# Writing out the order of stages 2 and 3 of a two-layer network in single engine steps

## The chip, the cores and the metric

The kernel runs on one core of one Trainium2 chip. The metric is the device time of one execution in microseconds (us). The core has five engines with instruction queues of their own: TensorE (PE: matmuls; PEld: its weight loads), VectorE (DVE), ScalarE (ACT), GpSimd (POOL) and SyncE (SP), which issues every DMA of this kernel. Each engine takes its instructions in the order in which they were put into its program, and an instruction whose input isn't there holds back all that stand behind it.

## What is computed

```python
def _A_ref(x, wqkv, wo):                      # linear attention, 32 heads of 18
    q, k, v = ...(x @ wqkv)
    phi = lambda t: jnp.where(t > 0, t + 1, jnp.exp(t)) + 1e-6
    pq, pk = phi(q), phi(k)
    kv = jnp.einsum("bhsd,bhse->bhde", pk, v)
    z = jnp.einsum("bhsd->bhd", pk)
    num = jnp.einsum("bhqd,bhde->bhqe", pq, kv)
    den = jnp.einsum("bhqd,bhd->bhq", pq, z)[..., None] + 1e-6
    return (num / den) @ wo
def _B_ref(x, w_q, k1, k2, u, v):             # 64 experts, one for each of 32 heads
    s1, s2 = (scores of x against the folded keys of both halves)
    i1, i2 = (the best of 8 in each)
    act = _gelu(x . u[i1 * 8 + i2])
    return sum over the heads of act * v[i1 * 8 + i2]
x = x + _A_ref(_layernorm(x)); x = x + _B_ref(_layernorm(x))
x = x + _A_ref(_layernorm(x)); x = x + _B_ref(_layernorm(x))
```

There are 2,048 tokens of 576 features, in float32. The same weights serve both layers.

## The kernel before

The tokens lie in 16 tiles of 128. All products are made in float32r, with each operand split into a high and a low part: ScalarE copies the high part, VectorE subtracts it (`split`, lines 117 to 120), and three products (high by high, high by low, low by high) are summed in PSUM, so that one product of a tile is 28 matmuls on TensorE. PSUM holds four buffers of two banks (line 70).

The work of a tile is cut into *pieces*, written as Python generators, and each piece into steps by `yield`. A piece has a short name (lines 756 to 775):

- `fT` (lines 300, 210 to 251): transposes the normalized tile for the front. Some tiles are transposed on TensorE (five transposes, then the split). The tiles in `SQUARES` (lines 57 to 61) go another way: VectorE transposes squares of 32, SyncE writes them to DRAM (line 233) and reads them back in four parts (line 239), then comes the split. `oT` (line 468) does the same for the attention's output, with one small GpSimd copy more (line 470), and `bT` (line 508) for the experts' input.
- `k`, `v`, `q` (lines 303 to 330): the front's three products with their evaluation. `keep` stores the transposed tile in DRAM, `rl` loads it back and `lq` makes the q product late (lines 332 to 349). `st` adds a tile's key-value state on TensorE (line 351).
- `mk`, `zs`, `M` (lines 379 to 433): after all 16 tiles, the state is masked and multiplied with the output weights (`wl` loads them).
- `ld` (`ldx`, `ldq`), `num`, `oT`, `O` (lines 436 to 492): load of x and q, division by the denominator, transposition, and the output product of 28 matmuls (line 485) with residual sum (line 475), and layernorm over GpSimd and ScalarE (lines 186 to 208).
- `bT`, `S` (lines 508, 520): transposition, and the experts' scores (14 matmuls of 512 columns, line 527). Its first matmuls need the high part of the transposed tile, its last five the low part. `sel` (line 550) picks the experts on VectorE, `gel` (line 535) makes the gelu on ScalarE and GpSimd.
- `cT`, `po` (lines 511, 600): transposition of the gates, and the experts' output product (four matmuls, line 609). In layer 1 `bc` (line 495) does a `bT` and the `cT` of another tile in one: up to six transposes, then one split for all. `base` (line 593) puts a residual into PSUM on TensorE.

Stage 1 (lines 778 to 858, about the first 148 us) is the front of layer 0 and the folding of the expert weights; its order is given by a loop. Stages 2 and 3 (lines 859 to 923) are written out as a text: `O1.2` means "the next step of piece `O` for layer 1, tile 2", `x3` means three steps, and `bc1.7,6` is the transposition of tile 7's input and tile 6's gates. `play` (line 767) runs such a text, and `in_order` (line 159) then ties each instruction of TensorE, ScalarE, VectorE and GpSimd to the one before it on its engine in the order of the text. The tie holds the order and is no semaphore. SyncE isn't among these: its transfers are put in order by the scheduler of the framework, by its own reckoning.

Of the kernel before, what the change touches and what calls it, by code (L numbers as in the profile page):

```python
# [22 lines left out]
P = 128  # L23
# [13 lines left out]
NB = 5  # L37
# [27 lines left out]
def network(ctx, tc, x_in, wqkv, wo, wq_t, k_t, u_t, v2, c_mask, c_mask4, c_ident, c_code, c_code1, c_scale, c_shift, out):  # L65
# [120 lines left out]
    def spread(xt, total, n):  # L186

        m = wk.tile([P, 2], F32, tag="mv", name=f"m{n}")
        nc.gpsimd.tensor_scalar(m[:, 0:1], total, -1.0 / D, 1.0, op0=ALU.mult, op1=ALU.mult)  # L189
        nc.scalar.activation(junk, xt, AF.Square, bias=m[:, 0:1], accum_out=m[:, 1:2])  # L190
        return m

    def layernorm_sum(xt, m, n):
# [3 lines left out]
        nc.gpsimd.tensor_tensor(rs[:, 1:2], m[:, 0:1], rs[:, 0:1], op=ALU.mult)  # L197
        return normalized(xt, rs, n)
# [11 lines left out]
    def transposed(y, n, more=None, tag="t", step=P):  # L210
# [16 lines left out]
    def moved(y, n, step=P):  # L227
# [3 lines left out]
        nc.vector.transpose(r.rearrange("p (j b c) -> p b j c", j=4, b=NB), at)  # L231
        d = dr.tile([P, NB * P], F32, name=f"y_d{n}")
# [9 lines left out]
    def squares(y, n, step=P):  # L242
        g = yield from moved(y, n, step)
        hi, lo = (wk.tile([P, NB, P], F32R, tag="t" + w, name=f"t{w}{n}", bufs=4) for w in ("hi", "lo"))
        yield
        split(g.rearrange("p q (b c) -> p b q c", b=NB), *(x.rearrange("p b (q c) -> p b q c", q=4) for x in (hi, lo)))
# [29 lines left out]
    def phi(p, n):  # L276
        e = wk.tile([P, D], F32, tag="e", name=f"e{n}", bufs=4)
        nc.scalar.activation(e, row(p), AF.Exp)  # L278
        nc.vector.tensor_scalar(e, e, 1.0, EPS, op0=ALU.min, op1=ALU.add)  # L279
# [3 lines left out]
    def phi_scalar(p, n):  # L283
# [4 lines left out]
        nc.scalar.activation(e, e, AF.Exp, scale=-1.0)  # L288
        nc.vector.scalar_tensor_tensor(e, e, EPS, row(p), op0=ALU.add, op1=ALU.add)  # L289
# [13 lines left out]
    def front_k(l, t):  # L303
# [4 lines left out]
        tt["fk", l, t] = (phi_scalar if l else phi)(k, f"k{l}_{t}")  # L308
# [15 lines left out]
    def front_q(l, t):  # L324
# [4 lines left out]
        fq = phi(q, f"q{l}_{t}")  # L329
        nc.sync.dma_start(pq_d[l][t], fq)  # L330

    def front_keep(l, t):

        hi, lo = tt["f", l, t]
        nc.sync.dma_start(hl_d[t][:, 0], hi.bitcast(F32))
        nc.sync.dma_start(hl_d[t][:, 1], lo.bitcast(F32))

    def late_load(l, t):
# [3 lines left out]
        nc.sync.dma_start(hi.bitcast(F32), hl_d[t][:, 0])  # L342
        nc.sync.dma_start(lo.bitcast(F32), hl_d[t][:, 1])
        tt["f", l, t] = hi, lo

    def late_q(l, t):
        q = product(tt["f", l, t], whi, wlo, 0, f"q{l}_{t}")
        yield
        tt["pq", l, t] = phi_scalar(q, f"q{l}_{t}")
# [16 lines left out]
    def wo_load(l, t):  # L366
# [7 lines left out]
        yield  # L374
# [4 lines left out]
    def state_mask(l, t):  # L379
        a = kva.pop(l)  # L380
        nc.scalar.activation(zc, a[:, :4 * 72 + 36], AF.Copy)
        for h in range(2):
# [63 lines left out]
    def back_load(l, t):  # L446
        back_x(l, t)
        back_pq(l, t)

    def back_scale(l, t):  # L450
# [7 lines left out]
        nc.vector.tensor_reduce(den, o[:, :D].rearrange("p (h e) -> p h e", h=H), axis=AX.X, op=ALU.add)  # L458
        nc.gpsimd.tensor_scalar(den, den, EPS, 1.0, op0=ALU.add, op1=ALU.mult)
# [4 lines left out]
                                r.unsqueeze(2).to_broadcast([P, H, DH]), op=ALU.mult)  # L464
        nc.gpsimd.tensor_copy(o[:, D:D + 56], o[:, D - 56:D])
        tt["o", l, t] = o

    def back_oT(l, t):
        hi, lo = tt["oT", l, t] = yield from turned("o", l, t, tt.pop(("o", l, t)), HC)
        nc.gpsimd.tensor_copy(lo[96:112, 4], hi[:16, 4].bitcast(F32))  # L470
# [7 lines left out]
    def back_out(l, t):  # L478
# [11 lines left out]
        m = spread(x1, total, "b" + n)  # L490
        yield
        ys["b", l, t] = layernorm_sum(x1, m, "b" + n)
# [18 lines left out]
    def exp_c(l, t):  # L511
# [5 lines left out]
        split(pt[:, :P], hi, lo)  # L517
        tt["c", l, t] = hi, lo

    def exp_scores(l, t):  # L520
# [8 lines left out]
        s = wk.tile([P, D], F32, tag="s", name="s" + n)  # L529
        nc.gpsimd.memset(s[:, :NE], 0.0)  # L530
# [437 lines left out]
```

## Time and profile before

| | |
|---|---|
| runs | 715.62 us median of 3 (715.54 to 719.01) |
| the profiled execution | 716.96 us, its span 715.1 us |
| granted TensorE clock | 0.997 of full speed (mean of the span) |
| busy: PE / DVE / ACT / POOL | 98% / 65% / 45% / 28% of the span |
| DMA | 107 MB, 150 GB/s mean |

The span is the time from the first instruction to the last. The profile's page gives each engine's busy time; the query of waits says how long an engine sat idle before an instruction and which instruction ended that; the timeline lists instructions by start time; windows give busy times by stretch; the chain lists what ended last, step by step. A busy time of PE includes the time that a matmul takes to run through, so a gap of some tenths of a microsecond between matmuls doesn't show as idle.

### The profile page before, as it was taken

To read this page: it belongs to the slowest core of one execution; us is meant where nothing else is said; L and a number is where in the kernel's file an instruction comes from. 1 tells how busy PE (TensorE), PEld (TensorE's weight loads), DVE (VectorE), ACT (ScalarE), POOL (GpSimd) and SP (SyncE) were. 2 spreads that over 40 slices of the span, in tenths; PEclk is the share of its full clock that TensorE was granted. 3 is DMA by queue.
4 is the path that set the end of the run, shared out by engine and by line. 5 is a ranking of instruction groups with operands and counts; after the bars stand their busy time and mean duration, and the time that the engine had idled before them with its cause. 6 is when DMAs were issued, how large, how long until landed. Compare 5 with 4: busy or idle time off the path is not lost.

```text
span 715.1 us, 14670 instructions
## 1 busy us (share of the span) xinstructions
PE 698.0 (98%) x5464; PEld 650.7 (91%) x5464; DVE 467.9 (65%) x1005; ACT 321.7 (45%) x658; POOL 202.4 (28%) x544
## 2 busy tenths in 40 slices
PE   9999999999999999999999999999999999999995
PEld 6999989999998899889998999999899999999984
DVE  5533342435436876688877888552647788987986
ACT  5422432343224547455555555544543544444443
POOL 2211000111004533333443433210224244433441
PEclk9999999999999999999999999999999999999998
DMA  9848878775302322566767675513632324121101
GB/s 269 293 153 255 267 229 264 247 196 176 108 1 53 114 91 93 166 209 210 233 207 241 216 220 175 165 53 100 176 98 82 123 71 137 45 73 34 67 17 66
DMA packets 82711, 107.17 MB, mean 150 GB/s; under 512 B 8976, under 2 KB 47376, under 8 KB 82640
## 3 DMA queue, kind: packets, MB, share of 16 engines
q1 hardware_dynamic: 82640, 106.24, 47.5%
q8 instruction: 43, 0.70, 0.4%
q14 instruction: 28, 0.23, 0.1%
HBM read 68.88 MB, written 37.32 MB: 149 GB/s over the span
## 4 chain that ended last, share of the span: by engine, by line
PE 79%; DVE 8%; ACT 4%; DMA 3%; issue 3%; POOL 1%; SPq 1%; DVEq 0%; ACTq 0%; POOLq 0%
PE ppq L260 15%; PE ppk L260 13%; PE ppo L485 13%; PE ppv L260 12%; PE pps L527 8%; PE kva L527 4%; PE kva L362 2%; PE fold_ps L641 2%; PE ptb L217 2%; PE po L609 2%; DMA go<-y_do 1%; PE m L416 1%; PE pto L217 1%; DVE x L475 1%; PE ppq L272 1%
## 5 line engine op out<-in xcount | busy, mean ns | idle before, releaser
L485 PE MATMUL ppo<-ohi,thio 126*128 126x252 f32 (+1 forms) x320 | 50.7, 301 | 4.5 <-ACT thio L119 4.4
L485 PEld LDWEIGHTS ppo<-ohi,thio 126*128 126x128 f32 (+1 forms) x320 | 44.9, 189 | 6.2 <-ACT thio L119 5.1
L260 PE MATMUL ppk<-whi,thif 128*128 128x252 f32 (+1 forms) x300 | 45.3, 298 | 0.8 <-ACT thif L119 0.8
L455 POOL TENSOR_TENSOR o<-pq,zb 128x576 f32<-128x576 f32 x19 | 27.4, 1443 | 62.5 <-ACT zb L401 58.7
L190 ACT ACTIVATE junk<-x,mb 128x576 bf16<-128x576 f32 x32 | 24.8, 775 | 45.0 <-POOL mb L189 44.9
L260 PE MATMUL ppv<-whi,thif 128*128 128x252 f32 (+1 forms) x300 | 44.7, 296 | 0.2 <-ACT thif L119 0.2
L260 PEld LDWEIGHTS ppk<-whi,thif 128*128 128x128 f32 x300 | 40.9, 188 | 4.0 <-issue 2.9
L181 POOL TENSOR_SCALAR rsf<-mvf 128x1 f32<-128x1 f32 x16 | 3.4, 212 | 145.3 <-DVE mvf L178 145.2
L207 ACT ACTIVATE yb<-x,rsb 128x640 f32<-128x640 f32 x32 | 29.5, 922 | 33.2 <-POOL rsb L197 33.2
L260 PE MATMUL ppv<-whi,tlof 128*128 128x252 f32 (+1 forms) x300 | 43.9, 293 | 0.0
L260 PE MATMUL ppk<-whi,tlof 128*128 128x252 f32 (+1 forms) x300 | 43.9, 293 | 0.0
L260 PEld LDWEIGHTS ppv<-whi,thif 128*128 128x128 f32 x300 | 41.4, 188 | 1.1 <-issue 0.4
L260 PEld LDWEIGHTS ppk<-whi,tlof 128*128 128x128 f32 x300 | 41.2, 188 | 0.0
L260 PEld LDWEIGHTS ppv<-whi,tlof 128*128 128x128 f32 x300 | 41.2, 188 | 0.0
L485 PE MATMUL ppo<-olo,thio 126*128 126x252 f32 (+1 forms) x256 | 39.6, 293 | 0.0
L260 PE MATMUL ppq<-whi 128*128 128x252 f32 (+1 forms) x260 | 39.5, 298 | 0.0
L485 PE MATMUL ppo<-ohi,tloo 126*128 126x252 f32 (+1 forms) x256 | 39.5, 293 | 0.0
L279 DVE TENSOR_SCALAR ek<-ek 128x576 f32<-128x576 f32 x16 | 7.3, 457 | 45.8 <-ACT ek L278 45.6
L260 PEld LDWEIGHTS ppq<-whi 128*128 128x128 f32 x260 | 36.0, 188 | 0.6 <-DVE eq L289 0.3
L485 PEld LDWEIGHTS ppo<-olo,thio 126*128 126x128 f32 x256 | 36.2, 188 | 0.0
L485 PEld LDWEIGHTS ppo<-ohi,tloo 126*128 126x128 f32 x256 | 36.1, 188 | 0.0
L260 PE MATMUL ppk<-wlo,thif 128*128 128x252 f32 x240 | 36.1, 293 | 0.0
(211 smaller groups left out, 1776.2 us busy)
## 6 DMA issues: line engine op xcount, KB each, us to landing
fold<-in_wq_t SPq DMA_DIRECT2D x64, 288.0 KB
whi<-hl_d SPq DMA_DIRECT2D x26, 320.0 KB
y_df<-rf SPq DMA_DIRECT2D x23, 320.0 KB
gf<-y_df SPq DMA_DIRECT2D x92, 80.0 KB
pq_d<-eq SPq DMA_DIRECT2D x19, 288.0 KB
pq<-pq_d SPq DMA_DIRECT2D x19, 288.0 KB
xf<-in_x SPq DMA_DIRECT2D x16, 288.0 KB
x<-in_x SPq DMA_DIRECT2D x16, 288.0 KB
```

The source lines that it names most:

```text
L190: nc.scalar.activation(junk, xt, AF.Square, bias=m[:, 0:1], accum_out=m[:, 1:2])
L207: nc.scalar.activation(y, x2, AF.Identity, scale=rs[:, 0:1], bias=rs[:, 1:2])
L217: nc.tensor.transpose(pt[:, b * P:(b + 1) * P], x, ident)
L260: nc.tensor.matmul(o[:, at:at + c1 - c0], tt[a == "lo"][:, b, :], wb[:, cols + c0:cols + c1], start=(i == 0), stop=(i == len(todo) - 1))
L272: nc.tensor.matmul(p[:, at:at + c1 - c0], tt[a == "lo"][:, b, :], wb[:, cols + c0:cols + c1], start=(i == 0), stop=(i == len(todo) - 1))
L279: nc.vector.tensor_scalar(e, e, 1.0, EPS, op0=ALU.min, op1=ALU.add)
L362: nc.tensor.matmul(a[64 * h:64 * h + 64, c * 72:c * 72 + n], vt[:, 2 * c + h], fk[:, f0:f0 + n], start=(t == 0 and c == 0), stop=(t == NT ...
L455: nc.gpsimd.tensor_tensor(o[:, :D], pq, zb, op=ALU.mult)
L485: nc.tensor.matmul(p[:, at:at + c1 - c0], hl[a][:r, b], w[:r, c0:c1], start=(i == 0), stop=(i == len(todo) - 1))
L527: nc.tensor.matmul(p[:, :512], hl[a == "lo"][:, b, :], shi[:, b] if w == "hi" else slo[:, blocks(REM)[b][1]], start=(i == 0), stop=(i == l ...
L609: nc.tensor.matmul(p[:, at:at + c1 - c0], c[i], vmix[:, c0:c1], start=(i == 0 and not based), stop=(i == 1))
L641: nc.tensor.matmul(p[32 * j:32 * j + 32, at:at + c1 - c0], kpad[:, ch // 2, 24 - 8 * a:56 - 8 * a], st[:, c0:c1], start=(a == 0), stop=(a ...
```

## The change

No instruction is added or taken away in stages 2 and 3; both texts order the same 1,673 steps (1,681 where the loads of the output weights are cut up too). What changes:

- Inside the pieces, more places to stop are marked with `yield 1`. They stand between the parts of different engines and between transfers: between ScalarE's and VectorE's part of a split, between each engine's part of `phi`, of the layernorms, of `num`, `gel` and `S`, between the two loads of `ld`, the two of `rl`, the two stores of `keep`, and the ten of `wl`. `run` skips these stops for stage 1 (`fine=False`) and uses them for the texts (`fine=True`). The two buffers of a split are asked for one step later.
- The three groups of texts (lines 861 to 923, one of them a loop over pairs of tiles) become one text without a loop, in a new order.
- `in_order` gets SyncE as a fifth engine: the transfers of stages 2 and 3 are issued in the order of the text.

```diff
+    def halved(src, hi, lo):
+        nc.scalar.activation(hi, src, AF.Copy)
+        yield 1
+        nc.vector.tensor_tensor(lo, src, hi.bitcast(F32), op=ALU.subtract)
...
     def transposed(y, n, more=None, tag="t", step=P):
...
+        yield
         hi = wk.tile([P, nb, P], F32R, tag=tag + "hi", name=f"thi{n}", bufs=4 if tag == "t" else 1)
         lo = wk.tile([P, nb, P], F32R, tag=tag + "lo", name=f"tlo{n}", bufs=4 if tag == "t" else 1)
-        yield
-        split(pt[:, :w], hi.rearrange("p a b -> p (a b)")[:, :w], lo.rearrange("p a b -> p (a b)")[:, :w])
+        yield from halved(pt[:, :w], hi.rearrange("p a b -> p (a b)")[:, :w], lo.rearrange("p a b -> p (a b)")[:, :w])
...
     def moved(y, n, step=P):
         nc.vector.transpose(r.rearrange("p (j b c) -> p b j c", j=4, b=NB), at)
+        yield 1
         d = dr.tile([P, NB * P], F32, name=f"y_d{n}")
         nc.sync.dma_start(d, r)
         yield
...
     def exp_scores(l, t):
...
+        yield 1
         nc.gpsimd.memset(s[:, :NE], 0.0)
         yield
...
-    def run(l, *seq):
+    def run(l, *seq, fine=False):
...
                 for i in range(n[0] if n else 99):
-                    if g is None or next(g, bc) is bc:
+                    e = bc if g is None else next(g, bc)
+                    while e == 1 and not fine:
+                        e = next(g, bc)
+                    if e is bc:
                         break
...
-    with in_order(*ALL):
+    with in_order(*ALL, ET.SP):
         play("""
...
-            num0.3 bT0.0 num0.4 oT0.2 O0.2 ld0.6 num0.3 bT0.0 O0.1 S0.0 num0.3 num0.4 q0.14 O0.1 oT0.3 O0.2 S0.0 bT0.1
...
-        for s in range(5, 13, 2):
-            play("""
-            bT0.0 num0.2 po0.-2 sel0.-1x3 gel0.-1 po0.-2x2 v1.-3 gel0.-1 v1.-3 k1.-3 bT0.0 fT1.-2 oT0.1 num0.2 ld0.3
-            sel0.-1 num0.2 k1.-3 bT0.0 fT1.-2 O0.1 cT0.-1 S0.0 O0.1 oT0.2 cT0.-1 po0.-1 O0.1 fT1.-2 num0.3 v1.-3
...
-            lq1.9 bc1.6,4 num1.15 O1.14 num1.9 oT1.8 S1.6 O1.14x2 sel1.5 O1.14 S1.6 gel1.5 po1.4 num1.15 sel1.5x2 O1.7
...
-            num1.12 O1.11 sel1.15 bc1.10,9 O1.11 oT1.12 S1.10 sel1.15 po1.9 O1.11 sel1.15 oT1.12 S1.10 gel1.10
-            bc1.11,15 sel1.10 O1.12 po1.9 gel1.10 bc1.11,15 O1.12x2 S1.11 sel1.10x2 po1.15 sel1.10 po1.15 S1.11
-            sel1.11 O1.12 sel1.11 base1.10 bc1.12,10x2 gel1.11x2 sel1.11 S1.12x2 sel1.11 base1.11 gel1.12 sel1.12
-            gel1.12 po1.10 bc1.-1,11x2 base1.12 sel1.12x2 po1.10 sel1.12 po1.11x2 bc1.-1,12x2 po1.12x2
...
+            O0.1 num0.3 ld0.4x2 oT0.2x4 bT0.0x3 S0.0 num0.3 S0.0 q0.14x2 O0.1x2 ld0.5 num0.3 O0.2 num0.4 num0.3x2
...
+            oT0.8 O0.8 sel0.6 cT0.6x2 k1.4 cT0.6 O0.8 oT0.9x2 O0.8 bT0.7 O0.8 bT0.7 O0.8 S0.7 po0.6x2 S0.7 fT1.5x2
+            po0.6x2 k1.5 num0.10 O0.8 v1.5 oT0.9 bT0.8x2 po0.6x2 S0.7 po0.6 sel0.7 gel0.7x4 oT0.9 fT1.6x2 sel0.7
+            num0.10 sel0.7 oT0.9x2 bT0.8 k1.5x2 fT1.6 sel0.7 bT0.8 ld0.11x2 O0.9 cT0.7 oT0.10x2 fT1.6 cT0.7 O0.9 bT0.8
...
+            O0.14x2 fT1.12x2 oT0.15 k1.11 cT0.13 oT0.15x2 cT0.13 O0.15 bT0.14 cT0.13 O0.15 bT0.14x2 S0.14 O0.15x2
...
+            q1.13 po0.15x3 v1.14x2 k1.14 q1.13x3 fT1.15 keep1.12 st1.13 fT1.15x2 k1.14 k1.15 v1.15 k1.15 rl1.2 k1.14
...
+            O1.1x2 lq1.3 num1.2x2 num1.13 oT1.13x3 bc1.0,-9 oT1.13 bc1.0,-9x2 S1.0x2 num1.2 S1.0 sel1.0 rl1.6x2 rl1.5
...
+            oT1.2x2 O1.2 sel1.0x2 O1.2 q1.14 O1.2 num1.4x2 num1.3 lq1.6 O1.2 O1.1 bc1.1,-9x2 num1.4 O1.13 bc1.1,-9
+            O1.2 S1.1x2 O1.2 gel1.0 sel1.0 bc1.2,0 lq1.6x2 S1.1 rl1.8x2 lq1.5 gel1.1x3 sel1.1x2 bc1.2,0 gel1.1 sel1.1
...
+            bc1.13,1 oT1.4x2 bc1.13,1 O1.3 bc1.13,1 S1.13 rl1.11 num1.6 po1.1 lq1.7 O1.3 bc1.3,2 S1.13x2 gel1.13
...
+            lq1.9 po1.1 po1.3 num1.15x2 bc1.6,4 num1.15 num1.8 bc1.6,4x2 S1.6 sel1.5 lq1.9 O1.14x2 oT1.7 gel1.5x3
...
+            O1.9 O1.8 oT1.15 ldx1.9 O1.9x3 gel1.14x3 bc1.7,6x2 sel1.14x2 bc1.7,6 S1.7x2 po1.6 po1.4 oT1.15x3 S1.7
...
+            gel1.15x2 sel1.15 sel1.10 gel1.10 O1.12x4 po1.9 gel1.10 po1.9 bc1.11,15 O1.12 bc1.11,15 sel1.10 gel1.10
+            po1.9 bc1.11,15 S1.11 gel1.10 po1.15 sel1.10 S1.11 po1.15 S1.11 sel1.11x2 O1.12 bc1.12,10 po1.15
+            bc1.12,10x2 S1.12x2 gel1.11 sel1.11 gel1.11 base1.12 gel1.11x2 base1.10 po1.10 sel1.11 bc1.-1,11 S1.12
+            gel1.12 sel1.12 bc1.-1,11 base1.11 bc1.-1,11 po1.11x2 gel1.12 sel1.12 gel1.12x2 po1.11 po1.10x2 sel1.12x2
+            bc1.-1,12x3 po1.12x3
```

More of the change, by code (lines that the diff above doesn't have):

```diff
@@ L516, in exp_c @@
         yield
-        split(pt[:, :P], hi, lo)
+        yield from halved(pt[:, :P], hi, lo)
         tt["c", l, t] = hi, lo
@@ L838, in network @@
                 first_load(0, 4)
-                first_ln(0, 3)
+                run(0, (ln, 3))
             else:
@@ L852, in network @@
             run(0, (k, t), (v, t, 1))
-            first_ln(0, t + 2)
+            run(0, (ln, t + 2))
             if done is not None:
@@ new lines, in network @@
+            gel0.3x2 po0.2 q0.10 O0.4 k1.1 oT0.6 k1.1 bT0.4x2 num0.5x2 oT0.5 v1.1 po0.2 oT0.5 ld0.7 keep1.0 oT0.6
+            sel0.3x2 k1.1 oT0.5 num0.7 oT0.6 num0.7 po0.2x3 v1.1 wl1.0 v1.1 gel0.3 bT0.4 S0.4 po0.2 S0.4 gel0.3
+            sel0.3x2 cT0.3 q0.14 keep1.1 oT0.5 O0.5 fT1.2 cT0.3x2 S0.4 sel0.4 O0.5 num0.7 gel0.4 po0.3 fT1.2 ld0.8
+            oT0.6 fT1.2 ld0.8 O0.5x2 oT0.6 gel0.4x2 po0.3x3 sel0.4 po0.3 O0.5 q0.13 st1.0 st1.1 O0.5 po0.3 sel0.4
+            bT0.5 gel0.4 sel0.4 num0.7 po0.3 bT0.5 fT1.3x2 bT0.5 v1.2x2 oT0.6 O0.6x2 num0.7 oT0.7 num0.8 cT0.4 v1.2
@@ new lines, in network @@
+            cT0.4x2 bT0.5 num0.8x2 oT0.7 O0.6x2 fT1.3 num0.8 bT0.5 O0.6 fT1.3 oT0.7 keep1.0 fT1.3 keep1.3 S0.5 k1.2
+            po0.4 S0.5x2 gel0.5 po0.4x2 O0.6 bT0.6 sel0.5 po0.4 gel0.5 sel0.5 po0.4x2 ld0.9 oT0.7 gel0.5 po0.4 fT1.4
+            bT0.6 oT0.7 gel0.5 sel0.5x2 num0.8 oT0.8 k1.2x2 v1.3x3 k1.3x2 oT0.7 O0.7 fT1.4 O0.7 ld0.9 bT0.6x2 cT0.5
+            num0.9 fT1.4 oT0.8 bT0.6 S0.6 keep1.3 S0.6 fT1.4 cT0.5x2 S0.6 fT1.4 po0.5x2 keep1.4 ld0.10x2 k1.3 po0.5
+            O0.7x2 po0.5x2 st1.2 O0.7x2 gel0.6 oT0.8 sel0.6 bT0.7x2 po0.5 gel0.6 num0.9 po0.5 gel0.6 fT1.5x2 oT0.8
@@ new lines, in network @@
+            po0.7x3 v1.5 po0.7 sel0.8 num0.11x2 po0.7 fT1.7 v1.6 gel0.8 fT1.7 keep1.6x2 bT0.9 oT0.10x3 v1.5 gel0.8x2
+            num0.11 fT1.7 sel0.8x3 k1.6x2 O0.10x2 ld0.12 O0.10 st1.4 st1.5 O0.10 k1.6 cT0.8 v1.6x2 cT0.8x2 bT0.9x2
+            S0.9 po0.8 num0.11 oT0.11 fT1.7 oT0.11 po0.8 fT1.7 O0.10x2 v1.7 k1.7 ld0.13 bT0.10 po0.8x2 S0.9 oT0.11
+            S0.9 sel0.9 po0.8x2 num0.12 po0.8 bT0.10 fT1.8x2 num0.12x2 oT0.11 num0.12 gel0.9 num0.12 sel0.9 ld0.13
+            oT0.11x2 k1.7 bT0.10x2 sel0.9 k1.7 fT1.8 gel0.9x3 oT0.12x2 ld0.14 keep1.7 O0.11 fT1.8 O0.11x3 sel0.9
```

148 lines of the change are left out of this document (86 added, 62 removed).

## The prediction

> **What bounds the kernel now.** I read the page first, for the engine that is never idle; then the windows, for where it idles all the same; then the query of waits for TensorE, for what ends those gaps; then the timeline around each.
>
> ```profile
> PE 698.0 (98%) x5464; PEld 650.7 (91%) x5464; DVE 467.9 (65%) x1005; ACT 321.7 (45%) x658; POOL 202.4 (28%) x544
> PE   9999999999999999999999999999999999999995
> PEclk9999999999999999999999999999999999999998
> ```
> ```profile
> 0.00:20.00 20.00, 18.51 (x104) 13.59 (x105) 12.32 (x21) 11.11 (x16) 5.35 (x14) 1.00 0.93 272
> 20.00:40.00 20.00, 19.80 (x179) 19.08 (x178) 10.46 (x20) 8.08 (x17) 5.08 (x14) 1.00 0.75 260
> 300.00:320.00 20.00, 17.36 (x134) 16.20 (x133) 16.64 (x36) 12.16 (x27) 7.09 (x20) 1.00 0.67 215
> 700.00:720.00 20.00, 8.26 (x36) 6.32 (x36) 8.48 (x25) 3.93 (x11) 3.02 (x9) 0.83 0.11 45
> ```
>
> TensorE works in 698.0 of 715.1 us, at full clock until the last slice. Of the 17.1 us idle, 1.5 and 0.2 lie in the first 40 us, which the change leaves alone, and 6.8 in the tail (700 to 715.1, 8.26 busy). So 8.6 us lie in between: all that a better order of stages 2 and 3 could win ahead of the tail. The change takes no matmul away. The time after is therefore the same TensorE work plus the gaps that the new order leaves, and I price only gaps.
>
> ```profile
> PE ppo L485 <- ACT thio L119: 4.4, 4, 1.4
> PE ptb L217 <- DVE cg L590: 2.5, 1, 2.5
> PE pps L527 <- ACT thib L119: 1.0, 1, 1.0
> PE ppk L260 <- ACT thif L119: 0.8, 1, 0.8
> PE po L609 <- DVE ek L289: 0.6, 1, 0.6
> PE kva L362 <- ACT g L541: 0.5, 1, 0.5
> ```
>
> The largest item is four waits of `O` for the high part of its transposed input. The 2.5 us belong to the tail.
>
> **Term 1, new gaps: a product right behind its own transposes.** In the new text nine `S` steps follow their own transposition with no TensorE step between: layer 0 tiles 0 and 14, layer 1 tiles 0, 1, 6, 7, 11, 12, 13 (`bT0.0x3 S0.0`; `bc1.7,6x2 sel1.14x2 bc1.7,6 S1.7x2`, where `sel` is VectorE's). In the old text this holds for `S1.12` alone; in the other eight a whole `O`, late product or `S` (3.2 us or more) stands between, for layer 0's tile 14 a state step and a transpose (0.9). TensorE is tied to the text's order, so nothing can slip into the gap: ScalarE has to copy the high part first. Two places of before show what that costs, and a third what the same transposes cost with ready work behind them:
>
> ```profile
> 159.40 0.71 PE L653 MATMUL fold_pt<-ident,foldf 128*128 128x128 f32 x5
> 159.86 1.57 PE L260 MATMUL ppv<-whi,thif 128*128 128x252 f32 x10
> ...
> 491.10 0.77 PE L217 MATMUL ptf<-ident,yf 128*128 128x128 f32 x5
> 491.90 0.70 ACT L119 ACTIVATE thif<-ptf 128x640 fp32r<-128x640 f32 x1 [0.90 <-PE ptf L217]
> 492.66 1.57 PE L260 MATMUL ppk<-whi,thif 128*128 128x252 f32 x10 [0.79 <-ACT thif L119]
> ...
> 698.35 0.53 PEld L217 LDWEIGHTS ptb<-ident,yb 128*128 128x128 f32 x5 [0.51 <-ACT yb L207]
> 698.35 0.77 PE L217 MATMUL ptb<-ident,yb 128*128 128x128 f32 x5
> 698.96 0.27 PE L217 MATMUL ptb<-ident,cg 128*128 128x128 f32 x1
> 699.32 0.81 ACT L119 ACTIVATE thib<-ptb 128x768 fp32r<-128x768 f32 x1 [1.02 <-PE ptb L217]
> 700.19 1.42 PE L527 MATMUL pps<-shi,thib 128*128 128x512 f32 x5 [0.96 <-ACT thib L119]
> ```
>
> From start to start, five transposes take 0.46 us with ready work behind them (159.40 to 159.86) and 1.56 us with their own product behind them (491.10 to 492.66): 1.1 us lost. Six take 1.84 us (698.35 to 700.19) where some 0.6 us (0.46 and a sixth's 0.1) would do: 1.2 us. Of the eight new places four have five transposes (layer 0 tiles 0, 14; layer 1 tiles 0, 1) and four have six: 4 x 1.1 + 4 x 1.2 = 9.2 us. By the idle times of the matmuls in brackets it would be 4 x 0.79 + 4 x 0.96 = 7.0; I take 9.2, as start to start holds the whole loss. Nothing covers this: were the copy queued behind other ScalarE work, it would only be longer.
>
> **Term 2, gaps that go.** `k1.15` gets the state step of tile 13 ahead of it (`fT1.15 keep1.12 st1.13 fT1.15x2 k1.14 k1.15`): its 0.8 goes. `po0.12` no longer stands directly behind its one transpose: 0.6. The state step that waited for an evaluation (0.5) gets over 10 us of other matmuls ahead of it. Together 1.9. `bT0.0` still has its layernorm's input too late; that stays.
>
> **Term 3, the four waits of `O`.** These lie where the tile goes through DRAM:
>
> ```profile
> 377.23 0.32 SPq L239 DMA_DIRECT2D go<-y_do  x1
> 377.64 0.38 SPq L617 DMA_DIRECT2D x_d<-x  x1
> 378.07 0.42 SPq L239 DMA_DIRECT2D go<-y_do  x1
> 378.59 0.42 SPq L233 DMA_DIRECT2D y_db<-rb  x1
> 379.06 2.49 SPq L239 DMA_DIRECT2D go<-y_do  x2
> ...
> 384.20 1.59 PE L485 MATMUL ppo<-ohi,thio 126*128 126x252 f32 x10 [1.22 <-ACT thio L119]
> ```
> ```profile
> 351.39 0.66 PE ppo L485 x3
> 379.53 3.77 DMA go<-y_do
> ...
> 384.20 0.92 PE ppo L485 x5
> ```
>
> The scheduler's order puts another tile's store and a write between the four reads of one transposition. The first read goes out at 377.23, the last at 379.5; what it brings lands 3.77 us on, ScalarE copies, and TensorE has idled 1.22 us. The new text issues the four reads as one step, and with SyncE tied nothing comes between. In the old loop no TensorE step lies between the reads and `O` for tiles 7, 9, 11 and 13; in the new text for 9 and 11 only. I follow tile 9: its reads stand behind the store of `po0.6`, whose residual sum ends about 0.8 us after that product, which is two products (7.3 us) ahead of `O0.9`. 0.8 + 0.4 (store) + 1.8 (four reads) + 3.2 to 3.8 (landing) + 0.8 (copy) = 7.0 to 7.6 us against 7.3. So it is just in time, and a few tenths of jitter show. Of the 4.4 us I let 3.7 go; bounds 0 and 4.4.
>
> **Term 4, the tail.**
>
> ```profile
> 689.73 3.94 PE ppo L485 x28
> 693.66 3.20 PE pps L527 x14
> ...
> 697.39 0.97 PE po L598 x4
> 698.36 0.89 PE ptb L217 x6
> ```
>
> From the end of the last `O` to tile 12's transposes there are 4.7 us, and TensorE's weight loads wait in them for the layernorm (0.51, the row at 698.35 above), although `base1.10` was put there. The new text moves `base1.10` behind `S1.12`, into the 2.5 us in which TensorE waits for the last `sel`, and puts tile 11's transposes and a `po` behind the last `O` in its place: the wait goes, counted as 0.4, and so does `base1.10`'s part of the path, 0.5 of the 0.97. From `S1.12` on the chain is that of before. Minus 0.9; bounds 0 and minus 1.0.
>
> **Edits at nothing.** The stops issue no instruction. The later request for the split's buffers changes which step asks, not when the copy may start. `first_ln` as steps issues the same instructions in stage 1.
>
> **The sum.** 9.2 - 1.9 - 3.7 - 0.9 = +2.7 us. Against the profiled execution: 716.96 + 2.7 = 719.7. That execution lay 1.3 us over the median of 715.62, so for the median I say 718.3. Lower end: 7.0 - 1.9 - 4.4 - 1.0 = -0.3, and about 2 us more if small waits that are no whole entry above go too: 713.3. Upper end: 9.2 - 1.9 = +7.3, all four waits staying or coming back elsewhere: 722.9. A measurement of this kernel can tell about 0.5% (3.6 us) from no change: faster means below 712.0, slower above 719.2.
>
> **Rival A, faster.** Many long pieces begin slowly: 28 matmuls took 3.94 us in the row above and 3.69 elsewhere.
>
> ```profile
> 287.67 3.69 PE ppo L485 x28
> ```
>
> If such quarters of a microsecond are short waits for operands that hide within "busy", finer steps could remove them. There are 98 such pieces in stages 2 and 3 (66 front products, 32 `O`); with 0.25 in half of them there would be 12 us to win, and nine tenths of it would give 718.3 - 11 = 707. Against it: the first ten matmuls took 1.57 us behind transposes that they don't depend on (159.86), and the same after a plain wait (492.66, and 1.59 at 384.20). So the slow start seems to belong to a change of kind, and any order has such changes. Chance 0.09.
>
> **Rival B, slower: SyncE becomes the bound in layer 0's middle.**
>
> ```profile
> L239 SPq DMA_DIRECT2D go<-y_do x40: 318/426/2012, 293.2 to 442.1; - x40
> 290.42 0.32 SPq L233 DMA_DIRECT2D y_do<-ro  x1
> 293.15 3.00 SPq L239 DMA_DIRECT2D go<-y_do  x4
> ```
>
> A tile there has 20 transfers on SyncE (three transpositions of five, two loads, two `keep`, one store of x) at 0.43 us: 8.6. A read directly behind its own write holds the queue for 293.15 - 290.42 - 0.32 = 2.4 us. Three such a tile make 15.8 us, and TensorE needs (384.20 - 351.39) / 2 = 16.4. Mostly the new text pairs them (write, write, read, read), so about two a tile: 13.4. But the order is fixed now: if a store of x waits for its residual sum at the head and the reads wait behind it, each such wait is added. From a fourth one of 2.4 us on (18.2) SyncE decides; in every second tile of ten that is 5 x 1.8 = 9 us less what buffers take up, say 6: 718.3 + 6 = 724.3. It would show as waits of `S`, `v` and `k` too. For it: tile 9 above is already just in time. Chance 0.18.
>
> [...]
>
> **Rival C, a gap long enough to lower TensorE's clock.** The clock was full beside gaps like that of 1.22 us at 384.20; in the last stretch, with a gap of 2.5 us and the idle end, the profile shows 0.83. If the tied SyncE queue makes one gap of some 4 us a few times, that gap itself costs 4 and some of the matmuls behind it run slower: three of them give 718.3 + 12 = 730 or more. Chance 0.03. [...]
>
> **Rival D, it doesn't do what it says:** the coarse pieces already let each engine run ahead within its own order, so finer stops may change nothing but the text, and the term 1 gaps are swallowed by waits that would be there anyway: 715.6. Chance 0.06.
>
> **How the numbers follow.** The forecast's own case has 0.64: its range of 713.3 to 722.9 lies mostly between 712.0 and 719.2 (0.47), the rest above (0.17). With rival D, within 0.5% is 0.53; faster 0.09 from A; more slower 0.17 + 0.18 + 0.03 = 0.38. The range from 712.5 to 724 leaves out A, C and the far half of B, some 2 in 10.
>
> **What would show it.** Right: in the waits of TensorE, `pps <- ACT thib` grows from one of 1.0 us to nine with 8 to 9 us; `ppo <- ACT thio` falls below 1; `ppk <- ACT thif` and `po <- DVE ek` vanish; TensorE's busy time stays at 698. Wrong: `pps` waits that stay at one (term 1 wrong), `ppo` waits of 4 us (term 3), SyncE waits followed by `ppv` or `pps` waiting for `thif` or `thib` from DRAM (rival B), a busy time of PE below 690 (rival A).

## The result and the profile after

The changed kernel takes **758.6 us** (median of 4 runs, 755.87 to 761.14), the kernel before 716.75 us in the runs beside it (715.54 to 719.01): a ratio of 1.058, 95% interval 1.053 to 1.063. It is slower by 41.9 us. The forecast was 718.3 with a range of 712.5 to 724.0. The profiled execution took 759.6 us, its span 757.8 us. Ratios and intervals leave out a run that lies far above the others of its kernel (here one alone, of 1766 us, in e15).

The page of the changed kernel, engines and slices:

```profile
PE 709.7 (94%) x5464; PEld 656.4 (87%) x5464; DVE 471.5 (62%) x1005; ACT 320.7 (42%) x658; POOL 203.0 (27%) x544
PE   8999999999999899799999999998899999989885
PEclk9999999999999999899999999999999999999998
```

The same 5464 matmuls take 709.7 us instead of 698.0: 11.7 us more. TensorE's idle time goes from 715.1 - 698.0 = 17.1 to 757.8 - 709.7 = 48.1: 31.0 us more. Together they are the 42.7 us of the two spans. So there are two things to explain, more gaps and slower matmuls, and the prediction had said that the busy time stays at 698.

The waits of TensorE in the changed kernel (time in total, how many, the longest):

```profile
PE pps L546 <- ACT thib L124: 11.9, 11, 2.3
PE kva L546 <- ACT thib L124: 9.5, 7, 4.4
PE ppq L269 <- DMA whi<-hl_d: 6.1, 2, 3.8
PE kva L546 <- DVE tlob L126: 3.4, 3, 1.5
PE pps L546 <- DVE tlob L126: 3.3, 3, 1.9
```

Four of these five groups were nowhere in the list of before. All but the third end at `S` (L546, which writes into `pps` or into the state's tile `kva`); the third is a reload of the late queries' inputs. The timeline has the single waits behind these groups, and they give a split that is used below: the eight places of the prediction's term 1 wait 9.1 us for their high part, the other `S` 11.4 us (the place that waited before, `S1.12`, 0.9), all `S` 6.7 us for their low part, and two reloads 6.1 us. `ppo <- ACT thio` (4.4 before) and `ppk <- ACT thif` (0.8) are gone, as forecast.

The worst of the gaps in layer 0, from the timeline of the changed kernel (start, duration, instruction, in brackets the idle time ahead of it and what ended it):

```profile
300.53 0.93 ACT L215 ACTIVATE yb<-x,rsb 128x640 f32<-128x640 f32 x1 [0.47 <-POOL rsb L204]
...
302.36 0.32 SPq L242 DMA_DIRECT2D y_db<-rb  x1
...
305.27 1.84 SPq L248 DMA_DIRECT2D gb<-y_db  x4
...
308.89 0.74 ACT L124 ACTIVATE thib<-gb 128x640 fp32r<-128x640 f32 x1 [3.27 <-DMA gb<-y_db]
...
309.69 2.50 PE L546 MATMUL kva<-shi,thib 128*128 128x512 f32 x5 [4.37 <-ACT thib L124]
311.99 1.91 PE L546 MATMUL kva<-slo,thib 128*128 128x512 f32 x4
313.69 1.94 PE L546 MATMUL kva<-shi,tlob 128*128 128x512 f32 x5
315.47 1.48 PE L269 MATMUL ppk<-whi,thif 128*128 128x252 f32 x10
```

This is `S0.5`. Its normalized row is ready at 300.53 + 0.93, is written to DRAM at 302.36, read back from 305.27 on, copied at 308.89, and TensorE has stood for 4.37 us. The tie isn't what makes this gap: in e1 below, where SyncE isn't tied, it is 4.77 us. Then fourteen matmuls take from 309.69 to 315.47, 5.8 us, where the fourteen of an `S` took 3.2 in before (the row of `pps L527 x14` in the prediction). The windows show this as a granted clock of 0.83 and 0.91 (the third number from the end; 1.00 in the windows of before that the prediction shows, but for the last, 0.83); from 309 to 316 us, which holds the fourteen, it is 0.57:

```profile
300.00:320.00 20.00, 15.63 (x90) 14.11 (x89) 9.48 (x18) 6.75 (x14) 5.20 (x16) 0.83 0.47 154
520.00:540.00 20.00, 14.70 (x86) 13.62 (x87) 5.14 (x11) 4.64 (x8) 1.85 (x3) 0.91 0.83 223
```

The gaps ahead of `S` have a second cause, which lies on ScalarE. At `S1.7` TensorE waits 2.34 us, though its transposes have started at 677.72. ScalarE takes up the copy only after another tile's layernorm pass, for which it waits itself:

```profile
679.05 0.78 ACT L197 ACTIVATE junk<-x,mb 128x576 bf16<-128x576 f32 x1 [0.99 <-POOL mb L195]
680.03 0.79 ACT L124 ACTIVATE thib<-ptb 128x768 fp32r<-128x768 f32 x1
```

The copies for `S1.11` (1.74 us), `S1.9` (2.03) and `S0.9` (1.87) stand behind other ScalarE work in the same way.

### The profile page after: what moved, and what is told of

Same layout as the page of the kernel before. It is cut to its first block, busy times and chain, and to the rows that moved or that the text cites. A ratio compares the mean times of both kernels' runs of the same rounds, so it can differ in the third digit from the quotient of the medians.

```text
span 757.8 us, 14610 instructions
## 1 busy us (share of the span) xinstructions
PE 709.7 (94%) x5464; PEld 656.4 (87%) x5464; DVE 471.5 (62%) x1005; ACT 320.7 (42%) x658; POOL 203.0 (27%) x544
## 5 line engine op out<-in xcount | busy, mean ns | idle before, releaser
L546 PE MATMUL pps<-shi,thib 128*128 128x512 f32 x105 | 30.4, 421 | 11.9 <-ACT thib L124 11.9
L187 POOL TENSOR_SCALAR rsf<-mvf 128x1 f32<-128x1 f32 x16 | 3.4, 213 | 141.8 <-DVE mvf L184 141.6
L494 DVE SCALAR_TENSOR_TENSOR x<-po,x 128x576 f32<-128x576 f32 x29 | 21.9, 755 | 28.3 <-PE po L631 27.8
```

The source lines that it names most:

```text
L187: nc.gpsimd.tensor_scalar(rs[:, 0:1], mv[:, 1:2], EPS_LN, 1.0, op0=ALU.add, op1=ALU.mult)
L494: nc.vector.scalar_tensor_tensor(y, row(p), 0.0, xt, op0=ALU.add, op1=ALU.add, accum_out=total)
L546: nc.tensor.matmul(p[:, :512], hl[a == "lo"][:, b, :], shi[:, b] if w == "hi" else slo[:, blocks(REM)[b][1]], start=(i == 0), stop=(i == l ...
```

## The experiments

Theories to tell apart. **A**: the written order puts too little other work between a step and the step that reads it (on TensorE, on VectorE, or round DRAM). It splits into **A1**, TensorE's order alone does it, and **A2**, the order of VectorE, ScalarE and GpSimd does it. **B**: SyncE, tied to the text, holds transfers up. **C**: part of the loss is TensorE's clock behind the gaps. "Us over" means over the kernel before in the runs beside it (716.8 to 717.6 us).

### SyncE: tied or not

```diff
-    with in_order(*ALL, ET.SP):     # the changed kernel
+    with in_order(*ALL):            # e1
...
-    with in_order(*ALL):            # the kernel before, second and third text
+    with in_order(*ALL, ET.SP):     # e2
```

> The changed kernel with the third text played without SyncE, so that the scheduler orders SyncE's transfers itself; TensorE, VectorE, ScalarE and GpSimd keep the written order. Theory A (the written order leaves too little other work on TensorE and VectorE between a step and the step that reads it, and the clock falls behind the long gaps): the gaps stay, 752 to 762 us, the waits of the S products for thib stay near 24 us together. Theory B (SyncE tied to the text holds writes and reads up behind others): most of the loss goes, 720 to 730 us, and the waits for thib fall by half or more.

> The kernel before with SyncE tied to the written order in its second and third text, all else as before. Theory A (the order on TensorE and VectorE): the old order has enough other work between the steps, so that a held-up SyncE is covered: 712 to 722 us. Theory B (tying SyncE is what costs): 735 us or more, with TensorE waiting for thib or for yb in the middle of the layers.

e1 took 752.26 us (ratio 1.047, 1.043 to 1.051): 6.3 less than the changed kernel, 7.9 by the two ratios. e2 took 722.71 (1.006, 1.004 to 1.008): 5.1 over. The tie costs 5 to 8 us, and theory B explains a seventh to a fifth of the loss. What goes in e1 is the wait for the reload. In the changed kernel the first late q product needs tile 0's halves (issued at 518.70 and 519.17). By the text they stand behind the first half of tile 2's (517.71), and SyncE holds that one for 8.6 us, until the front's last value product (`ppv`) is through:

```profile
517.71 0.38 SPq L355 DMA_DIRECT2D whi<-hl_d  x1
...
518.70 0.43 SPq L355 DMA_DIRECT2D whi<-hl_d  x1
519.17 0.52 SPq L357 DMA_DIRECT2D whi<-hl_d  x1
522.95 2.57 PE L269 MATMUL ppq<-whi 128*128 128x252 f32 x10 [3.76 <-DMA whi<-hl_d]
```

and in e1, where the scheduler issues tile 0's halves first, the same product starts without a wait and at full pace:

```profile
520.63 1.59 PE L269 MATMUL ppq<-whi 128*128 128x252 f32 x10
```

### The smaller steps without the new order

The new frame (one text, all the new stops), but the text spells out the old order of the four compute engines, and SyncE isn't tied:

```diff
-            num0.3 bT0.0 num0.4 oT0.2 O0.2 ld0.6 num0.3 bT0.0 O0.1 S0.0
+            num0.4 oT0.2x3 O0.2 ld0.6x2 num0.3x2 bT0.0x2 O0.1x2 S0.0x2
```

> The changed kernel's smaller steps and its single text, but with the text holding the order of the kernel before, step by step, on TensorE, VectorE, ScalarE and GpSimd; SyncE not tied. Theory A (the order is what costs, not the smaller steps nor the frame they are played in): 715 to 721 us, as before. Rival (smaller steps allocate buffers at other moments and so cost by themselves): 730 us or more.

718.25 us, ratio 1.0015 (0.9997 to 1.0032). The stops and the frame cost nothing that can be told from no change. So the order is the cause: 34 us between this kernel and e1, which differ in the order of the four compute engines alone, and the tie's 5 to 8. From here on this kernel, called the old order in steps, is the base for single features.

### Mending the new order one engine at a time

e3 moves ten TensorE steps up, e17 moves `S` down in eight places, both on TensorE alone:

```diff
-  lq1.10 O1.9 oT1.15 bc1.7,6 S1.7     (TensorE's steps, the changed kernel)
+  lq1.10 bc1.7,6 O1.9 oT1.15 S1.7     (e3)
...
-  bc1.7,6 S1.7 po1.6 lq1.11
+  bc1.7,6 po1.6 lq1.11 S1.7           (e17, SyncE not tied)
```

> The changed kernel with ten TensorE steps moved, so that another TensorE step lies between the transposes of an S product and the product in nine places; the other engines' order and SyncE's are as they were. Theory A: term 1 of the prediction goes nearly whole, some 10 us, and 1 to 3 us of slow clock behind the gaps with it: 745 to 750 us, pps<-thib below 5 us. Theory B (SyncE): within 3 us of 758.6.

> The changed kernel with SyncE not tied (752.3 us), and the eight S products moved down on TensorE by one product or a short step (or that step moved up), so that something stands between the transposes and S; the other engines keep the new order. If the gap of term 1 can be taken out of the new order on TensorE alone: 740 to 745 us. If a later S makes the steps that hang on it late, since the other engines' order was written around it (as in the run with ten steps moved): 750 us or more.

e3 took 781.54 us, 23 more than the changed kernel; e17 764.43, 12 more than e1. Both are misses for the simple reading of theory A. The waits of e3:

```profile
PE pps L546 <- ACT thib L124: 10.5, 6, 2.5
PE ptb L225 <- ACT yb L215: 9.2, 5, 3.6
PE ptb L225 <- DVE cg L612: 7.2, 4, 2.5
```

The transposes now wait themselves: 9.2 us for the normalized row where the changed kernel has 1.0, and 7.2 for `cg` where it has 2.5. In the text, the steps that make these stand where the later transposes needed them.

e4 moves VectorE's low parts up, directly behind ScalarE's high parts:

```diff
-  bT0.10 (hi) sel0.9 (s3) k1.7 (phi) oT0.12 (tr) O0.11 (res) sel0.9 (s4) bT0.10 (lo)
+  bT0.10 (hi) bT0.10 (lo) sel0.9 (s3) k1.7 (phi) oT0.12 (tr) O0.11 (res) sel0.9 (s4)
```

> The changed kernel with VectorE's low-part step of each transposition right behind ScalarE's high-part step in the text, so that it no longer stands behind VectorE's other steps (one tile, layer 1's tile 3, keeps its place). TensorE's, ScalarE's and SyncE's orders are as they were. Theory A in its part on the low parts: the waits of S for tlob (kva<-tlob, pps<-tlob, 6.7 us in the profile) and part of those put down to thib go, 748 to 752 us. Theory B (SyncE), and a theory that only TensorE's own order counts: within 2 us of 758.6.

772.83 us, 14 more: a miss as well. VectorE waits at the moved step (first row, VectorE's waits in the changed kernel; second, in e4), and what stands behind it comes late to TensorE (third, e4):

```profile
DVE tlob L126 <- ACT thib L124: 3.5, 6, 0.8
```
```profile
DVE tlob L126 <- ACT thib L124: 24.8, 14, 4.5
```
```profile
PE pto L225 <- DVE o L480: 7.0, 2, 3.9
```

### Whose order is it?

Two kernels hold only TensorE to the text and leave the other engines to the scheduler:

```diff
-    with in_order(*ALL):
+    with in_order(ET.PE):     # e7 with the old text in steps, e8 with the new text
```

> The old order in smaller steps again, but only TensorE is held to the text in stages 2 and 3; the scheduler orders VectorE, ScalarE, GpSimd and SyncE itself. It is the partner of the next kernel. If TensorE's order alone sets the time: 715 to 725 us. If the order of the other engines matters as much: 735 us or more.

> The changed kernel with only TensorE held to its text; the scheduler orders VectorE, ScalarE, GpSimd and SyncE itself. Theory A1 (TensorE's new order leaves too short a way from a product to the product that needs its outcome, whatever the others do): 745 us or more, and 25 us or more above its partner with the old order of TensorE. Theory A2 (the new order of VectorE, ScalarE and GpSimd is what holds steps up): within 10 us of its partner.

859.8 and 878.52 us. Leaving the other engines to the scheduler costs 141.6 us under the old text and 126.3 under the new one, so this surrounding is too far off to judge TensorE's order in. The two lie 18.7 us apart, between the 10 of A2 and the 25 of A1, which settles nothing.

Two mixtures do better. Written side by side, TensorE's old and new orders differ in 38 short stretches. e10 is the old order in steps with TensorE's new order in 26 of them (the other 12 can't be had without a change on another engine); e11 is the new order, SyncE not tied, with TensorE's old order in 25. Two state steps of e10 (layer 1's tiles 3 and 4) come after the value rows of tiles 5 and, in part, 6 have been written over theirs, so e10 computes other sums; the amount of work is the same.

> The two written orders of TensorE split into 38 short stretches in which the same steps stand in another order. Here the old order in smaller steps (718.3 us), with TensorE's new order in 26 of the 38 stretches; VectorE, ScalarE and GpSimd keep their old order exactly, SyncE is not tied. Theory A1 (TensorE's order carries the loss): 735 us or more. Theory A2 (the order of VectorE, ScalarE and GpSimd carries it): 717 to 726 us.

> The mirror of the run before: the new order on VectorE, ScalarE and GpSimd exactly, SyncE not tied (752.3 us with TensorE's new order), and TensorE's old order in 25 of the 38 stretches. Theory A1: 735 us or less. Theory A2: 745 us or more.

764.42 us (ratio 1.067, 1.062 to 1.071) and 800.11 us (1.115, 1.112 to 1.119): each mixture is slower than both orders that it is made of, the old one in steps (718.25) and the new one without the tie (752.26). If A1 held, e11 would have come down; if A2 held, e10 would have stayed. Both fall in the form in which I put them. The waits of e10, then of e11:

```profile
PE ptb L225 <- ACT yb L215: 10.0, 7, 3.6
PE ppo L504 <- ACT thio L124: 9.5, 8, 1.7
```
```profile
PE pps L546 <- ACT thib L124: 9.2, 7, 2.7
PE pto L225 <- DVE o L480: 7.1, 2, 4.0
```

They are spread over inputs of every kind. In these four orders the price of one engine's order depends on the others'.

### Building the loss up from the old order

So the features of the new text were put into the old order in steps, where the surroundings are sound. First, term 1 of the prediction alone (TensorE's steps, one of eight places):

```diff
-  lq1.3 bc1.0,-9 O1.1 S1.0
+  lq1.3 O1.1 bc1.0,-9 S1.0
```

> Term 1 of the prediction alone: the old order in smaller steps, with the TensorE steps that stood between the transposes of eight S products and the products (layer 0 tiles 0, 14; layer 1 tiles 0, 1, 6, 7, 11, 13) moved ahead of the transposes or behind the product, so that each S stands right behind its transposes. The other engines keep their old order. By the prediction's term 1: 718.3 + 9 = 727 us. Rival (the gap is given back, since TensorE then waits less elsewhere): 722 us or less.

730.48 us (ratio 1.019, 1.016 to 1.021): 12.2 over the old order in steps. Waits of e12:

```profile
PE pps L546 <- ACT thib L124: 6.9, 8, 1.0
PE ptb L225 <- DVE cg L612: 4.7, 4, 2.5
```

Against the base's profile (`pps <- thib` 1.0, `cg` 2.5) these are seven new waits of `S` with 5.9 us; the eighth, `S0.14`, waits 0.8 into `kva`, and `cg` 2.2 us more. Little was given back: `O`'s waits for its high part fell from 5.0 us in the base's profile to 2.9.

Second, the low parts (the order of VectorE's steps; eleven of the thirteen move behind at least one other VectorE step, the expectation said ten):

```diff
-  bc1.2,0 (hi) bc1.2,0 (lo) sel1.1 (s2) sel1.1 (s3) S1.2
+  bc1.2,0 (hi) sel1.1 (s2) sel1.1 (s3) bc1.2,0 (lo) S1.2
```

> The old order in smaller steps, with VectorE's low-part step of thirteen transposes (those that stand behind other VectorE steps in the new text) moved down to right ahead of the S that reads it, behind one to three VectorE steps in ten of them. The other engines keep their old order. If late low parts alone cost what the waits of the changed kernel show: 725 us or more. If they cost only together with the rest of the new order: 717 to 722 us.

727.43 us (1.014, 1.011 to 1.017): 9.2 over the base. Waits of e13:

```profile
PE pps L546 <- DVE tlob L126: 3.8, 5, 1.2
PE po L631 <- DVE tlob L126: 2.4, 3, 1.6
```

Third, both:

> The two runs before in one: the old order in smaller steps with both the S products right behind their transposes and the low parts late. If the costs of the two (12.2 and 9.2 us over the 718.3 of the old order in smaller steps) add up: 737 to 743 us. If they overlap, since both end in the same waits of S: below 734 us.

739.14 us (1.031, 1.028 to 1.034). 718.25 + 12.2 + 9.2 = 739.7: they add up.

Fourth, less work over the way round DRAM:

```diff
-  v1.2 k1.2 O0.6 cT0.4 S0.5 po0.4
+  v1.2 O0.6 cT0.4 S0.5 k1.2 po0.4
```

> The old order in smaller steps with one step moved: the key product of layer 1's tile 2 goes behind S of layer 0's tile 5 (its two steps on ScalarE and VectorE with it), as the new text has it, so that 3.7 us less TensorE work lies between that tile's output product and its S, between which its normalized row goes to DRAM and back. If the gap of 4.4 us that the changed kernel has there comes from this, and the slow matmuls behind it cost extra: 721 to 725 us. If the transfer is early enough in the old order: 717 to 720 us.

728.05 us, ratio 1.0144 (1.011 to 1.018), 0.0129 over the base's: 9.3 us. The price is above what I expected, and the places are others. It is not `S0.5` that waits but `O0.6`, whose own input goes round DRAM too and which now starts one product earlier; and then, 25 us later, the engines round `O0.7`:

```profile
302.65 2.59 PE L504 MATMUL ppo<-ohi,thio 126*128 126x252 f32 x10 [5.02 <-ACT thio L124]
305.03 1.80 PE L504 MATMUL ppo<-olo,thio 126*128 126x252 f32 x8
...
319.37 0.75 DVE L300 SCALAR_TENSOR_TENSOR ek<-ek,ppk 128x576 f32<-128x576 f32 x1 [2.89 <-ACT ek L298]
...
327.79 1.31 PE L504 MATMUL ppo<-ohi,tloo 126*128 126x252 f32 x8 [1.54 <-DVE tloo L126]
...
330.73 1.40 PE L376 MATMUL kva<-ek,v 128*64 128x72 f32 x20 [1.36 <-DVE ek L300]
...
332.18 2.48 PE L546 MATMUL kva<-shi,thib 128*128 128x512 f32 x5
```

The first place has 5.02 us of idle time against 1.38 in the base, and 2.59 + 1.80 us for eighteen matmuls that took 1.59 + 1.20 there: 3.6 us of gap for a product of 3.7 us taken out of the cover of a DRAM round trip, and 1.6 us of slow matmuls. That is 5.2 us. The second place costs about as much again, and it isn't a round trip: VectorE now waits 2.89 us for the moved key product's evaluation, and behind it `O0.7`'s low part and the next evaluation come late (1.54 and 1.36 us), with a slow `S0.6` after them (2.48 us for its first five matmuls, where those of `S0.5` in the same trace took 1.40).

Fifth, all of it, and the second part of the text (from layer 0's tile 5 on) with SyncE tied:

> The old order in smaller steps with four features of the new text put in: the eight S products behind their transposes, the thirteen late low parts, the key product behind S of tile 5, and SyncE tied to the text (from layer 0's tile 5 on). If the causes add up: 718.3 + 12.2 + 9.2 + 3 to 6 + 5 = 748 to 751 us, so most of the 758.6 of the changed kernel. If something else in the new order carries the loss: below 742 us.

755.49 us (1.054, 1.051 to 1.057), above the 748 to 751 of the expectation, which had 3 to 6 for the fourth part. With its measured 9.3 the sum of the parts is 718.25 + 12.2 + 9.2 + 9.3 + 5.1 = 754.1. The four features put into the old order make it 38.3 us slower than the kernel before, where the changed kernel loses 41.9. e16's page and its longest group of waits:

```profile
PE 708.0 (94%) x5464; PEld 655.7 (87%) x5464; DVE 471.0 (62%) x1005; ACT 321.4 (43%) x658; POOL 201.9 (27%) x544
PE ppo L504 <- ACT thio L124: 12.7, 6, 5.0
```

The size is that of the changed kernel and the busy time nearly so (708.0 against 709.7). The places are not the same throughout: `O` waits 12.7 us for its high part here and not at all in the changed kernel, where `S` and the reload wait instead. So the nearness in size doesn't show that these four features make up the loss of the changed kernel; it shows that they can cost that much.

### The clock

e9 and e18 fill the longest gaps with matmuls that compute nothing (58 in six places, 74 in eight), in the PSUM tile that the product then overwrites:

```diff
+    FILL = {(0, 5): 16, (1, 7): 9, (1, 10): 8, (1, 11): 7, (1, 12): 4, "q1_0": 14}
...
         todo = passes(REM)
+        for i in range(FILL.get((l, t), 0)):
+            nc.tensor.matmul(p[:, :512], shi[:, 0, :P], shi[:, 0], start=True, stop=True)
```

> The changed kernel with 58 matmuls that compute nothing of use put ahead of six products that wait long (S of layer 0's tile 5, S of layer 1's tiles 7, 10, 11, 12 and the first late q product), in the products' own PSUM tiles, which the products then overwrite. They take about 0.26 us each, as long together as the gap that each group fills, so that TensorE doesn't stand still there. Theory C (the gaps cost twice, since the clock falls behind them; in the profile PE's busy time is 11.7 us longer): the work behind these gaps runs at full pace, 748 to 754 us. Rival (the long busy times are not the clock's doing but work that waits in TensorE's own queue): 758 us or more.

> The changed kernel itself once more, beside the next one on the same chip, so that the two can be compared to a few microseconds: 756 to 761 us.

> As the run with six filled gaps, with two more: 7 matmuls ahead of S of layer 0's tile 9 and 9 ahead of the second late q product, 74 in all. Theory C (behind a long gap the matmuls run at about half pace for some microseconds): 5 to 8 us under the changed kernel beside it, and the matmuls behind the former gaps at 0.26 us each. Rival (the clock costs nothing that counts): within 2 us of it.

e9 took 754.26 us, just above theory C's 748 to 754 and under the rival's 758. Side by side, the changed kernel took 759.62 (1.059, 1.056 to 1.062) and e18 752.5 (1.049, 1.046 to 1.052): 7.1 us less with 74 matmuls more. `S0.5` in e18:

```profile
305.13 3.92 PE L549 MATMUL kva<-shi 128*128 128x512 f32 x16
310.37 1.45 PE L551 MATMUL kva<-shi,thib 128*128 128x512 f32 x5 [1.32 <-ACT thib L124]
```

The high part comes no sooner (310.37 against 309.69), but the fourteen matmuls now end some 1.8 us sooner (the next product starts at 313.72 instead of 315.47). In e18's profile TensorE is busy for 718.3 us, of which the 74 added matmuls are 19.2 (7.5 + 5.9 + 5.8 by the list of groups). The kernel's own matmuls are back at 699.1, from 707.6 in the profile of the changed kernel beside it. The mean granted clock of the two profiled executions was 0.988 for the changed kernel and 0.997 for e18. Theory C holds: about 7 us of the loss are slow matmuls behind gaps.

## Why the prediction was wrong

**Term 1 was right in kind and a little small.** It said 9.2 us for eight places, 7.0 by idle times alone; in the changed kernel their idle times are 9.1. Six wait 0.79 to 0.90 us, as forecast, and `S1.7` and `S1.11` 2.34 and 1.74, because their copies are queued behind other ScalarE work: the case that the term named and put at nothing. So it is partly luck that 9.1 lies so near 9.2. Put into the old order the eight cost 12.2, of which 2.2 are a wait for `cg` that the term did not have.

**Terms 2 and 3 were right where they looked.** `ppk <- thif`, the four `ppo <- thio` and the wait of the state step are gone from the list; of term 2, the 0.6 of `po <- DVE ek` came back at a transpose (`ptc <- DVE ek`, 0.6). But term 3 took the four waits as gone for good. In the new order another way round DRAM is short of cover, as the 4.37 us at `S0.5` show.

**Term 4 was wrong.** The wait for `yb` ahead of the last transposes was to go. On the weight loads, where the term read 0.51 us, it grew to 1.20:

```profile
739.29 0.53 PEld L225 LDWEIGHTS ptb<-ident,yb 128*128 128x128 f32 x5 [1.20 <-ACT yb L215]
739.29 0.77 PE L225 MATMUL ptb<-ident,yb 128*128 128x128 f32 x5 [0.97 <-ACT yb L215]
741.07 1.99 PE L546 MATMUL pps<-shi,thib 128*128 128x512 f32 x5 [0.90 <-ACT thib L124]
```

`S1.12` behind it ran slowly (1.99 us for its first five matmuls; the granted clock from 739 to 745 us was 0.72), but not in the second profile of the same kernel, e19 (1.42 us).

**The step that failed** is the sentence "The time after is therefore the same TensorE work plus the gaps that the new order leaves, and I price only gaps", in both halves. The time of the work did not stay the same (709.7 us for 698.0). And the only new gaps priced were those between neighbours on TensorE: a product that stands directly behind its transposes. These are 9.1 us of the waits. For each `S` I counted the bare copy of the high part on ScalarE, and neither what stands ahead of it there nor the way round DRAM: the other `S` wait 11.4 us for their high part. I did not count the low part on VectorE, which the new text puts behind other VectorE steps: 6.7 us (9.2 in e13). And the reload on the tied SyncE, 6.1 us, was in no term. For the tiles that go round DRAM I checked one `O` and no `S`, though the key product of layer 1's tile 2 (3.7 us), which lay over `S0.5`'s way in the old order, had moved behind it. That its place makes the 4.37 us there is argued from the order and not shown: in e15 the same move cost 9.3 us, at other places. Beyond term 1, the upper end of 722.9 held only waits that were already in before.

**Rival B had the price, not the weight.** It said 6 us for a tied SyncE; the tie costs 5.1 on the old order and 6.3 on the new. On the new order most of it is the reload of the late queries, not layer 0's middle, where I had put it; that the size is so near is luck.

**Rival C came nearest**, with a chance of 0.03 and 730 us or more. Its terms were right: a gap of some 4 us (my estimate; before, no wait of TensorE was longer than 2.52), and slower matmuls behind it (5.8 us for the fourteen of `S0.5` instead of 3.2, 2.57 for the first ten of the late q product instead of 1.59). But there are two such gaps, 4.37 and 3.76 us, and only the second comes from the tied SyncE; the first stays without the tie. Most of the new idle time lies in the many shorter waits, which no rival had.

**What stays open.** How the loss of the changed kernel divides among its causes is read from its waits; the prices of e12 to e16 are those of the old order, and those of e15 lie at places where the changed kernel doesn't wait. Why each mixture is slower than both its parents is read from waits only: a step moved alone meets inputs that aren't there yet. Shown is that the features can be added to the old order at a price that adds up, and that three tries to take one out of the new order on one engine (e3, e4, e17) made it slower; a mended new order on all engines at once was not tried. No kernel here beats the one before.

## What to carry to other kernels

When an order is written out for several engines, go through every link from a product back to the product that feeds it, both halves of a split and the way round DRAM included, and count the other work that lies over it, old text against new; a count of neighbours on the busiest engine found less than a quarter of the loss. Count also what stands ahead of each link on its own engine, the queue of transfers included. Price each missing microsecond of cover at itself, and add something for the clock: here slow matmuls stood behind the five waits of 3.69 to 5.02 us listed below, and behind some of 0.90 to 2.33 us. Here such prices added up (754.1 summed, 755.49 measured). Expect that a fault in such an order isn't mended on one engine alone: none of three tries did it.

## What the runs showed of the hardware

In these runs the slow matmuls don't follow from the length of the gap alone. Two executions of the changed kernel were profiled, and the matmuls behind the same waits ran differently in them. First the rows of `S0.9`, `S1.7` and `S1.9` from the profile used so far, then from that of e19:

```profile
383.31 2.50 PE L546 MATMUL kva<-shi,thib 128*128 128x512 f32 x5 [1.87 <-ACT thib L124]
680.87 1.45 PE L546 MATMUL pps<-shi,thib 128*128 128x512 f32 x5 [2.34 <-ACT thib L124]
703.58 2.04 PE L546 MATMUL pps<-shi,thib 128*128 128x512 f32 x5 [2.03 <-ACT thib L124]
```
```profile
382.82 1.43 PE L546 MATMUL kva<-shi,thib 128*128 128x512 f32 x5 [1.87 <-ACT thib L124]
679.74 2.50 PE L546 MATMUL pps<-shi,thib 128*128 128x512 f32 x5 [2.33 <-ACT thib L124]
703.86 1.42 PE L546 MATMUL pps<-shi,thib 128*128 128x512 f32 x5 [2.03 <-ACT thib L124]
```

Behind each of the three gaps the matmuls were slow in one execution (2.50, 2.50 and 2.04 us for five) and at full pace in the other (1.43, 1.45 and 1.42). In the profile used so far the granted clock was 0.83 in the 10 us from 380 and in the 10 us from 700, which hold `S0.9` and `S1.9`, and 1.00 from 677 to 690, which holds `S1.7`. The gap before it didn't decide this either. e9 and e18 both fill the gap at `S1.7`, and behind the same 2.03 us at `S1.9` the five matmuls took 2.19 us in e9 and 1.45 in e18:

```profile
698.67 2.19 PE L551 MATMUL pps<-shi,thib 128*128 128x512 f32 x5 [2.03 <-ACT thib L124]
```
```profile
698.87 1.45 PE L551 MATMUL pps<-shi,thib 128*128 128x512 f32 x5 [2.03 <-ACT thib L124]
```

That wait of 2.03 us stands in all four of these traces; the matmuls behind it were slow in two (the changed kernel, e9) and at full pace in two (e18, e19). In five places a longer wait, of 3.69 us or more, has slow matmuls behind it:

| wait ahead of | us | the matmuls behind it |
|---|---|---|
| `S0.5`, the changed kernel | 4.37 | five in 2.50 us; 1.45 in e18 |
| first late q product, the changed kernel | 3.76 | ten in 2.57 us; 1.59 in e1, without a wait |
| `O0.6`, e15 | 5.02 | ten in 2.59 us; 1.59 in the kernel before |
| `O0.6`, e16 | 5.02 | the eight of `ppo<-olo,thio` in 1.58 us; 1.20 in the kernel before |
| `O0.7`, e16 | 3.69 | the eight of `ppo<-olo,thio` in 2.14 us; 1.20 in the kernel before |

Slow matmuls stood behind shorter waits too: behind 1.87, 2.03 and 2.33 us in the rows above, and behind the 0.90 us ahead of `S1.12`. Why they did in one execution and not in another, no run here settles. In the slow rows of this document the groups of four and five matmuls of 512 columns took 0.39 to 0.50 us a matmul; at full pace it is 0.26 to 0.29.
